# Moving and thinning the denominators' additions in the first attention of a fused attention and feed-forward kernel

## The chip, the core and the metric

The kernel runs on one core of a Trainium2 chip. A core has a matrix engine (TensorE, PE in the profile), a vector engine (VectorE, DVE), a scalar engine with table functions (ScalarE, ACT), a general engine (GpSimd, POOL) and SyncE (SP), which here only issues DMAs. Each engine takes its instructions in the order of its own list and meets the others through semaphores. The metric is device time in microseconds, the median of the runs. Lower is better.

## What is computed

There are 8 batches, 12 heads, 448 positions and a head dimension of 64. Queries and keys are normalised by their root mean square, and a softmax attention follows. Its output, 3584 tokens by 768, goes through a feed-forward layer of width 2048 with squared ReLU:

```
q_n, k_n = rmsnorm(q, g_q), rmsnorm(k, g_k)
attn = softmax(q_n @ k_n.T / sqrt(64)); x = attn @ v
h = x @ w_in; r = max(h, 0); out = (r * r) @ w_out
```

The two weight matrices come as 64-bit floats. The kernel turns them into 32-bit floats itself.

## The kernel before

**Stages.** The batches are taken two at a time, as a span. A span is one attention over 12 head pairs and then two products, each done as seven smaller block products in place of eight. The attention of a later span is woven into the second product of the span before it. Only the first attention (`attention_alone`) has no product to hide in: it stands alone at the start, and the first product of span 0 follows it.

**A head pair.** Each of the 12 pairs (`NAT`) goes through these steps. `load` brings q and k in from DRAM. `norm` squares them (ACT, L693), sums them (DVE, L694 and L695), takes the power -1/2 (POOL, L697) and multiplies q by it (POOL, L699). `transpose` turns k and then q on the PE (tile `pt`, L737), and ACT copies each result out (L739 for k, L741 for q). `scores` makes a chunk of 112 keys against all queries for both heads (PE, tile `sc`, L749), and ACT takes the exponential (L754). There are four chunks, 0 to 3. `values` multiplies the chunks by v (PE, tile `pav`, L805).

**The denominators.** The softmax needs the sum of the exponentials over the keys. `add_up` adds chunk 1 to chunk 0 and then chunk 2 to that (DVE, L764, 112 by 896 elements). `total_of` lets the PE multiply this sum, and each chunk that was not added, by a matrix of ones (tile `tot`, L815), which sums over the partitions. With three chunks added there are two operands, with two there are three. Each operand takes two matmul instructions, which the profile shows as four records. `finish` transposes the total, takes its reciprocal, transposes back and multiplies it into `pav` (DVE, L828, L829, L830, L835). `combine_x` makes the differences that the block products need (L845 to L850).

**The order.** It is written out by hand: each engine's list is the order in which the functions are called. In a pair the PE runs scores 0 and 1, the transpose of the next pair's k, the values of the pair before for chunks 2 and 3, the total of the pair before, the transpose of the next pair's q, scores 2 and 3, and the values for chunks 0 and 1.

**The weights' ticks.** At every `yield` of the attention the loop calls `weights`, which advances the conversion of the weights. One word of weights takes a tick of four quarters: a load (SP, L532), vector work (DVE, L588, L593, L598), scalar work (ACT, L575, L591), integer additions (POOL, L563) and block sums (POOL, L569). After every second word its seven blocks are written to a DRAM scratch of 1344 KB (`w1s`, SP, L583). `EARLY` says how many quarters are done by the end of the attention. The first product streams its stationary blocks `sw` back from that scratch (SP, L646); the first five of these loads are issued near the end of the attention, all on SP's one queue:

```
weights(min(EARLY, 4 + (EARLY - 4) * u // (4 * NAT - 7)))
if u == 4 * NAT - 9:
    load_blocks(5)
```

**Buffers.** `qk` holds two pairs of alternating parity, so `load(i + 3)` overwrites what `norm(i + 1)` has read. `tot` has one bank of PSUM, `pav` has two that alternate, and `pt` shares the bank of its predecessor: the transpose of q waits until ACT has copied the transpose of k.

Of the kernel before, what the change touches and what calls it, by code (L numbers as in the profile page):

```python
# [310 lines left out]
def load_q(nc, qk, q, i):  # L311

    _, H, S, D = q.shape
    b, h0 = divmod(2 * i, H)
    nc.sync.dma_start(places_of(qk, i, 0)[:S // 4, 0].rearrange("p (h e) -> p h e", h=2),
                      q[b, h0:h0 + 2].rearrange("h (p j) d -> p h (j d)", j=4))


def load_k(nc, qk, k, i):

    _, H, S, D = k.shape
    b, h0 = divmod(2 * i, H)
    dst = places_of(qk, i, 0)[:S // 4, 1].rearrange("p (j h d) -> p j h d", j=4, h=2)
    for h in range(2):
        nc.sync.dma_start(dst[:, :, h], k[b, h0 + h].rearrange("(p j) d -> p j d", j=4))
# [61 lines left out]
def attention_then_ffn_bounded(  # L387
# [41 lines left out]
    NJ = 4  # L429
    SP = S // NJ  # L430
    NPAIR = H // 2
    NFC = DFF // P
# [6 lines left out]
    NAT = 2 * NPAIR  # L439
# [16 lines left out]
    def bank(name, n=None):  # L456

        turn[0] += n is None
        return ps_m.tile([P, S], F32, tag="mn"[turn[0] % 2 if n is None else n], name=name)
# [22 lines left out]
    HW = HC * P  # L482
    WORDS, BLOCKS, EXPS = 7, 2, 4

    EARLY, ALL = 4 * 12, 4 * (2 * NFC + 3)
    assert DM == NW and BLOCKS * 8 * HW + EXPS * NW + 2 * NW <= 3 * HF * S and 2 * NW <= 4 * S and HF % 4 == 0


# [162 lines left out]
    vs, probs, pavs, tots, normed, rstds = {}, {}, {}, {}, {}, {0: rstd0}  # L651
# [3 lines left out]
    def load(i):  # L655
        if i < NAT:
            load_q(nc, qk, q, i)
            load_k(nc, qk, k, i)
            return

        b, h0 = i // NPAIR, 2 * (i % NPAIR)
        for s, src in enumerate((q, k)):
            dst = by_squares(i, 0)[:, s]
            for n in range(4):
                nc.sync.dma_start(dst[n * 32:(n + 1) * 32],
                                  src[b, h0 + n // 2, :, n % 2 * 32:n % 2 * 32 + 32]
                                  .rearrange("(g t) e -> t g e", t=32))

    def by_squares(i, work):
        n = i % 2 * 4 + 2 * work  # L670
        flat = qk[:, n:n + 2].rearrange("p n e -> p (n e)")[:, 0:2 * S]
        return flat.rearrange("p (s g e) -> p s g e", s=2, e=32)
# [11 lines left out]
    def norm(i):  # L684
        if i >= NAT:
            squares(i)
            return norm_by_squares(i)
        raw, sq = (places_of(qk, i, n)[:SP] for n in range(2))
        rstd = rstds[i] = small.tile([SP, 2, 2 * NJ], F32, tag="rstd", name="rstd", bufs=4)
        normed[i] = sq[:, 0], raw[:, 1]  # L690
        if i <= 2:
            return normalise_in_turn(nc, raw, sq, rstd, mhalf)
        nc.scalar.activation(sq, raw, AF.Square)  # L693
        nc.vector.tensor_reduce(rstd, sq.rearrange("p s (n d) -> p s n d", d=D), AX, ALU.add)  # L694
        nc.vector.tensor_scalar(rstd, rstd, 1.0 / D, 1e-6, ALU.mult, ALU.add)  # L695
        flat = rstd.rearrange("p s n -> p (s n)")
        nc.gpsimd.tensor_tensor(flat, flat, mhalf[:SP, 0:4 * NJ], ALU.pow)  # L697

        nc.gpsimd.tensor_tensor(sq[:, 0].rearrange("p (j h d) -> p h j d", j=NJ, h=2),  # L699
                                raw[:, 0].rearrange("p (h j d) -> p h j d", j=NJ, h=2),  # L700
                                rstd[:, 0].rearrange("p (h j) -> p h j ()", h=2).to_broadcast([SP, 2, NJ, D]),
                                ALU.mult)
# [30 lines left out]
    def transpose(i, s, n):  # L733

        pt = bank("pt", n)
        for j in range(NJ):
            nc.tensor.transpose(pt[:, j * SP:(j + 1) * SP], normed[i][s][:, j * P:(j + 1) * P], ident[:SP, :SP])  # L737
        if s:
            nc.scalar.copy(qkT[:, i % 2, s], pt)  # L739
        else:  # L740
            nc.scalar.activation(qkT[:, i % 2, s], pt, AF.Copy, scale=gains[:, 0:1])  # L741

    def scores(i, c):

        at = i % 2 if i < NAT else 0
        sc = ps_s.tile([SP, 2, 512], F32, tag="s", name="sc")
        for h in range(2):
            rows = slice(h * D, (h + 1) * D)
            nc.tensor.matmul(sc[:, h, 0:S], qkT[rows, at, 1, c * SP:(c + 1) * SP], qkT[rows, at, 0, :],  # L749
                             start=True, stop=True)  # L750
        pr = probs[i, c] = places[(NJ * i + c) % len(places)][:SP]
        if i < NAT:
            for h in range(2):
                nc.scalar.activation(pr[:, h], sc[:, h, 0:S], AF.Exp, scale=rstds[i][:, 1, 2 * c + h:2 * c + h + 1])  # L754
        else:
            nc.scalar.activation(pr, sc[:, :, 0:S], AF.Exp)  # L756

    def acc_of(i):
        return sums[i % 2] if i < NAT else sums["acc"]

    def add_up(i, c):

        acc = acc_of(i)[:SP]
        nc.vector.tensor_tensor(acc, probs[i, 0] if c == 1 else acc, probs[i, c], ALU.add)  # L764
# [35 lines left out]
    def values(i, chunks=range(NJ)):  # L800
        if 0 in chunks:
            pavs[i] = ps_o.tile([P, S], F32, tag="o", name="pav") if i >= NAT or i % 2 == 0 else bank("pav", 1)
        for c in chunks:
            for h in range(2):
                nc.tensor.matmul(pavs[i][h * D:(h + 1) * D, :], vs[i][:, h, c, :], probs[i, c][:, h, :],  # L805
                                 start=(c == 0), stop=(c == NJ - 1))

    def total_of(i):


        tots[i] = ps_o.tile([P, S], F32, tag="t", name="tot")
        parts = [acc_of(i)[:SP]] + [probs[i, c] for c in range(2 if i + 1 == NAT else 3, NJ)]
        for n, pr in enumerate(parts):
            for h in range(2):
                nc.tensor.matmul(tots[i][h * D:(h + 1) * D, :], sums["ones"], pr[:, h, :],  # L815
                                 start=(n == 0), stop=(n + 1 == len(parts)))

    def finish(i):

        b, hp = divmod(i, NPAIR)  # L820
        pav, factors = pavs.pop(i), xT[:, b % 2, hp]
        x = factors
        if i < NAT:


            turned, factors = sums["turned"], sums["factors"]
            few = small.tile([P, S // 32], F32, tag="few", name="few", bufs=1)
            nc.vector.transpose(turned, tots.pop(i))  # L828
            nc.vector.reciprocal(few, turned.rearrange("p (g r) -> p g r", r=32)[:, :, 0])  # L829
            nc.vector.transpose(factors.rearrange("p (g r) -> p g r", r=32),  # L830
                                few.rearrange("p g -> p g ()").to_broadcast([P, S // 32, 32]))

            x = x.rearrange("d (p j) -> d j p", j=NJ)
            pav, factors = (t.rearrange("d (j p) -> d j p", j=NJ) for t in (pav, factors))
        nc.vector.tensor_tensor(x, pav, factors, ALU.mult)  # L835
        del vs[i]
# [15 lines left out]
    def attention_alone():  # L852


        for i in range(NAT):
            more = i + 1 < NAT
            scores(i, 0)
            scores(i, 1)
            if i == 0:

                transpose(1, 1, 1)
                scores(0, 2)
                scores(0, 3)
                transpose(1, 0, 0)
                add_up(0, 1)
                add_up(0, 2)
                norm(2)
                load_v(1)
                values(0, (0, 1))
                load(3)  # L870
                yield
                continue
            if more:
                transpose(i + 1, 1, 0)
            if i + 3 < NAT:
                load(i + 3)
            values(i - 1, (2, 3))
            total_of(i - 1)
            add_up(i, 1)
            if i + 2 < NAT:  # L880
                norm(i + 2)
            elif not more:
                norm(NAT)
                load(NAT + 2)
            yield
            if more:
                transpose(i + 1, 0, 0)
            finish(i - 1)
            load_v(i + 1)
            yield  # L890
            scores(i, 2)
            scores(i, 3)
            values(i, (0, 1))
            yield
            if more:
                add_up(i, 2)
            combine_x(i - 1)
            if NAT <= i + 3 < NAT + 2:
                load(i + 3)
            yield  # L900
        values(i, (2, 3))
        total_of(i)
        finish(i)
        combine_x(i)
# [212 lines left out]
    for span in range(NSPAN):  # L1117
        more = span + 1 < NSPAN
# [108 lines left out]
```

## Time and profile before

| quantity | value |
|---|---|
| median of 3 runs | 1402.11 us (1399.25 to 1402.90) |
| the profiled execution | 1404.63 us |
| its span, first to last instruction | 1402.80 us |
| PE busy | 1378.1 us, 98% of the span |
| DVE, ACT, POOL busy | 814.3, 420.3, 590.7 us |
| first score matmul | 8.96 us |
| first matmul of the first product (tile `pa`) | 134.48 us |
| first score matmul of the second attention | 266.31 us |

Times inside the trace are counted from the span's start. In a row of the timeline the columns are start, duration, engine, line, operation, output and inputs, shape, count, and in brackets the engine's idle time before it with what ended it. Rows of equal instructions are merged with an x and a number. A share of busy time says little by itself; what counts is which wait ends last in each stage. From 266 us on the PE has no idle time, so the two stages before that are where the order of work can be seen in the time.

### The profile page before, as it was taken

The numbers are of one execution on the slowest core, as the hardware profiler recorded it, in microseconds if no ns is written. First come the engines' busy times: TensorE is split into PE (matmuls) and PEld (weight loads), VectorE is DVE, ScalarE is ACT, GpSimd is POOL, SyncE is SP. The second block draws the span as 40 slices with busy tenths as digits, with TensorE's granted clock in tenths as the row PEclk, the third lists the DMA queues.
The fourth block names the chain that finished last, engine by engine and source line by source line (L and its number), as shares of the span: only waits on it lengthen the run. The fifth ranks groups of instructions, "written<-read, shape, count | busy, mean of one in ns | idle before, by whom it ended". The sixth has DMA issues, their size and how long they took to land.

```text
span 1402.8 us, 14398 instructions
## 1 busy us (share of the span) xinstructions
PE 1378.1 (98%) x4426; PEld 635.5 (45%) x4426; DVE 814.3 (58%) x1404; ACT 420.3 (30%) x621; POOL 590.7 (42%) x400
## 2 busy tenths in 40 slices
PE   8989999999999999999999999999999999999997
PEld 3333444444444454544444455444444445554553
DVE  6989677589876234476767523457777633332111
ACT  7875555433322011233232011232323201110000
POOL 6998888544452022544353122445445302221000
PEclk9999999999999999999999999999999999999999
DMA  8676998645655333345565332344565343323443
GB/s 239 190 196 168 352 374 316 183 104 119 137 113 120 98 88 87 104 103 122 117 136 122 95 96 85 103 105 105 120 128 107 94 102 86 90 86 103 107 110 70
DMA packets 430914, 188.78 MB, mean 135 GB/s; under 512 B 277484, under 2 KB 428780, under 8 KB 430828
## 3 DMA queue, kind: packets, MB, share of 16 engines
q1 hardware_dynamic: 421228, 179.05, 49.3%
q10 hardware_dynamic: 9472, 8.72, 2.3%
q8 instruction: 37, 0.61, 0.2%
q14 instruction: 49, 0.40, 0.1%
q0 software_dynamic: 128, 0.00, 0.0%
HBM read 154.54 MB, written 33.16 MB: 134 GB/s over the span
## 4 chain that ended last, share of the span: by engine, by line
PE 89%; POOL 3%; DVE 3%; issue 1%; DMA 1%; ACT 1%; POOLq 0%; ACTq 0%
PE ps L1044 37%; PE pc L997 10%; PE pd L997 10%; PE pa L997 10%; PE sc L749 9%; PE pav L805 9%; PE pb L997 5%; DMA sw<-w1s 1%; DVE gT L764 1%; POOL rstd L697 1%; POOL gC L569 1%; POOL qk L699 1%; POOL gC L563 1%; DVE gC L598 0%; PE tot L815 0%
## 5 line engine op out<-in xcount | busy, mean ns | idle before, releaser
L1044 PE MATMUL ps<-gT,sw 128*128 128x448 f32 x768 | 299.2, 542 | 0.8 <-POOL gT L974 0.8
L719 POOL TENSOR_TENSOR half<-half,mhalf 128x28 f32<-128x28 f32 x36 | 173.6, 4824 | 262.3 <-DVE half L718 228.8
L1044 PE MATMUL ps<-gC,sw 128*128 128x448 f32 x576 | 225.2, 542 | 0.0
L974 POOL TENSOR_TENSOR gT<-gT 128x448 f32<-128x448 f32 x96 | 93.5, 976 | 311.9 <-ACT gT L970 311.9
L1044 PEld LDWEIGHTS ps<-gT,sw 128*128 128x128 f32 x768 | 143.9, 190 | 151.0 <-issue 146.5
L756 ACT ACTIVATE pr<-sc 112x896 f32<-112x896 f32 x120 | 104.8, 914 | 293.9 <-PE sc L749 201.7
L749 PE MATMUL sc<-qkT 64*112 64x448 f32 x768 | 171.5, 565 | 1.9 <-ACT gT L754 1.1
L1044 PEld LDWEIGHTS ps<-gC,sw 128*128 128x128 f32 x576 | 108.0, 190 | 112.3 <-issue 111.1
L997 PE MATMUL pa<-xT,sw 128*128 128x448 f32 x384 | 154.9, 539 | 0.5 <-DMA sw<-w1s 0.5
L970 ACT ACTIVATE gT<-gT 128x448 f32<-128x448 f32 x96 | 55.3, 576 | 312.6 <-DVE gT L1012 312.6
L749 PEld LDWEIGHTS sc<-qkT 64*112 64x112 f32 x768 | 61.2, 173 | 99.6 <-issue 81.5
L997 PEld LDWEIGHTS pa<-xT,sw 128*128 128x128 f32 x384 | 72.8, 190 | 72.5 <-issue 71.9
L805 PE MATMUL pav<-pr,vt 112*64 112x448 f32 x480 | 100.2, 547 | 0.0
L721 POOL TENSOR_TENSOR qk<-qk,half 128x448 f32<-128x448 f32 x72 | 84.3, 1191 | 2.8
L997 PE MATMUL pb<-xC,sw 128*128 128x448 f32 x192 | 77.6, 540 | 2.0 <-issue 1.5
L1012 DVE TENSOR_TENSOR gT<-z,pd 128x448 f32<-128x448 f32 x32 | 19.9, 621 | 102.2 <-PE pd L997 102.2
L764 DVE TENSOR_TENSOR acc<-acc,pr 112x896 f32<-112x896 f32 x60 | 68.3, 1138 | 18.4 <-ACT pr L756 15.9
L997 PE MATMUL pd<-xC,sw 128*128 128x448 f32 x192 | 77.5, 540 | 1.4 <-DMA sw<-w1s 1.3
L997 PE MATMUL pd<-xT,sw 128*128 128x448 f32 x192 | 78.0, 542 | 0.0
L997 PE MATMUL pc<-xC,sw 128*128 128x448 f32 x192 | 77.4, 539 | 0.0
L997 PE MATMUL pc<-xT,sw 128*128 128x448 f32 x192 | 77.4, 539 | 0.0
L569 POOL TENSOR_TENSOR gC<-gC 128x384 f32<-128x384 f32 x64 | 72.1, 1146 | 2.5
(120 smaller groups left out, 1565.7 us busy)
## 6 DMA issues: line engine op xcount, KB each, us to landing
sw<-w1s SPq DMA_DIRECT2D x224, 192.0 KB, 2.4
sw<-w2s SPq DMA_DIRECT2D x168, 256.0 KB, 3.3
w1s<-gC SPq DMA_DIRECT2D x8, 1344.0 KB, 7.5
w2s<-gC SPq DMA_DIRECT2D x8, 1344.0 KB, 5.7
out_dram<-osb SPq DMA_DIRECT2D x184, 56.0 KB, 1.9
qk<-in_q_dram SPq DMA_DIRECT2D x144, 56.0 KB, 3.0
qk<-in_k_dram SPq DMA_DIRECT2D x144, 56.0 KB, 2.9
vt<-in_v_dram SPq DMA_DIRECT2D x72, 112.0 KB, 2.9
```

What stands on the lines that cost most here:

```text
L569: nc.gpsimd.tensor_tensor(*[blocks_of(n)[:, i] for i in (dst, x, y)], op)
L719: nc.gpsimd.tensor_tensor(half, half, mhalf, ALU.pow)
L721: nc.gpsimd.tensor_tensor(qkn[:, s], raw[:, s], half[:, s * NG:(s + 1) * NG].rearrange("p g -> p g ()").to_broadcast([P, NG, 32]), ALU.mult)
L749: nc.tensor.matmul(sc[:, h, 0:S], qkT[rows, at, 1, c * SP:(c + 1) * SP], qkT[rows, at, 0, :], start=True, stop=True)
L756: nc.scalar.activation(pr, sc[:, :, 0:S], AF.Exp)
L764: nc.vector.tensor_tensor(acc, probs[i, 0] if c == 1 else acc, probs[i, c], ALU.add)
L805: nc.tensor.matmul(pavs[i][h * D:(h + 1) * D, :], vs[i][:, h, c, :], probs[i, c][:, h, :], start=(c == 0), stop=(c == NJ - 1))
L970: nc.scalar.activation(g, src, AF.Relu)
L974: nc.gpsimd.tensor_tensor(g, g, g, ALU.mult)
L997: nc.tensor.matmul(ps, stream[n + i][:, c], rhs[:, c], start=first and c == 0, stop=c == HC - 1, skip_group_check=not first)
L1012: add(g, x, ps, ALU.add)
L1044: nc.tensor.matmul(ps, stream[n][:, c % 4], rhs_of[i][:, c], start=c == 0, stop=c == HF - 1)
```

## The change

In the first attention, the DVE adds chunks 0 and 1 only for even pairs and for the last one, and chunks 0, 1 and 2 for the odd pairs; before, it added three chunks for all pairs but the last. The PE takes the third operand of `total_of` for those pairs. The total of a pair now comes after the next pair's scores 2 and 3, where it came before that pair's transpose of q, and `finish` follows after the values of chunks 0 and 1. The load of q and k three pairs ahead is called at the top of a pair. Thirteen ticks of the weights are done by the end of the attention instead of twelve.

```diff
-    EARLY, ALL = 4 * 12, 4 * (2 * NFC + 3)
+    EARLY, ALL = 4 * 13, 4 * (2 * NFC + 3)
...
+    def added(i):
+        return 3 if i % 2 and i + 1 < NAT else 2
+
     def total_of(i):
         tots[i] = ps_o.tile([P, S], F32, tag="t", name="tot")
-        parts = [acc_of(i)[:SP]] + [probs[i, c] for c in range(2 if i + 1 == NAT else 3, NJ)]
+        parts = [acc_of(i)[:SP]] + [probs[i, c] for c in range(added(i), NJ)]
...
             more = i + 1 < NAT
+            if 0 < i < NAT - 3:
+                load(i + 3)
             scores(i, 0)
             scores(i, 1)
...
                 add_up(0, 1)
-                add_up(0, 2)
                 norm(2)
...
                 transpose(i + 1, 1, 0)
-            if i + 3 < NAT:
-                load(i + 3)
             values(i - 1, (2, 3))
-            total_of(i - 1)
             add_up(i, 1)
...
                 transpose(i + 1, 0, 0)
-            finish(i - 1)
             load_v(i + 1)
             yield
             scores(i, 2)
             scores(i, 3)
+            total_of(i - 1)
             values(i, (0, 1))
+            finish(i - 1)
             yield
-            if more:
+            if added(i) == 3:
                 add_up(i, 2)
             combine_x(i - 1)
```

## The prediction

> **What bounds the kernel now.** I read the shares first, then the slices by stage, the waits of the first attention, the chain of waits, and the timelines of POOL and PE there. The page's shares and slices:
>
> ```profile
> PE 1378.1 (98%) x4426; PEld 635.5 (45%) x4426; DVE 814.3 (58%) x1404; ACT 420.3 (30%) x621; POOL 590.7 (42%) x400
> PE   8989999999999999999999999999999999999997
> ```
>
> PE is idle for only 24.7 us, nearly all in the first slices. The busy times by stretch (length, then each engine's time with its count, granted clock, DMA share, GB/s) say who competes with it there:
>
> ```profile
> 60.00:80.00 20.00, 19.50 (x104) 7.38 (x102) 19.73 (x25) 16.79 (x28) 19.69 (x13) 1.00 0.65 186
> 100.00:120.00 20.00, 16.48 (x82) 5.90 (x82) 19.13 (x27) 12.55 (x22) 19.68 (x12) 0.95 0.54 148
> 160.00:180.00 20.00, 19.52 (x52) 9.52 (x51) 15.18 (x20) 9.83 (x15) 17.18 (x18) 1.00 1.02 375
> 220.00:240.00 20.00, 20.00 (x55) 10.10 (x54) 14.03 (x18) 13.80 (x22) 16.84 (x18) 1.00 0.91 337
> ```
>
> In the attention PE, DVE and POOL are all full: a balance of three. In the first product the DMAs are full and PE waits little. The waits from 10 to 135 us (total, times, longest):
>
> ```profile
> PE tot L815 <- DVE gT L764: 4.4, 5, 1.5
> PE pt L737 <- POOL qk L699: 2.2, 2, 2.0
> PE sc L749 <- ACT gT L754: 1.1, 1, 1.1
> PE pav L805 <- DMA vt<-in_v_dram: 0.9, 1, 0.9
> ```
>
> The first row is what the change goes for. But the chain of waits, taken from 60 us on, is held by POOL from 67 to 116.5 us; its end is
>
> ```profile
> 110.71 3.06 POOL rstd L697
> 113.85 2.65 POOL qk L699
> 116.50 0.04 issue
> 116.55 0.60 PE pt L737 x4
> 117.15 2.26 PE sc L749 x8
> 119.41 2.73 PE pav L805 x8
> ```
>
> So the last multiplication of a norm (pair 11) releases the last transpose, and from there PE runs to the product at 134.48. POOL has three idle spells from 25.7 to 116.5 us: 0.54, 1.12 and crumbs. Its rows, and DVE's additions, show what fills it:
>
> ```profile
> 46.37 2.90 POOL L697 TENSOR_TENSOR rstd<-rstd,mhalf 112x16 f32<-112x16 f32 x1
> 49.36 1.04 POOL L699 TENSOR_TENSOR qk<-qk,rstd 112x512 f32<-112x512 f32 x1
> 69.88 1.86 POOL L699 TENSOR_TENSOR qk<-qk,rstd 112x512 f32<-112x512 f32 x1
> ```
>
> ```profile
> 70.74 1.95 DVE L764 TENSOR_TENSOR gT<-gT 112x896 f32<-112x896 f32 x1
> 78.22 1.07 DVE L764 TENSOR_TENSOR gT<-gT 112x896 f32<-112x896 f32 x1
> ```
>
> An addition takes 1.07 us alone and up to 1.98 beside POOL's elementwise work; POOL's multiplication takes 1.04 alone and up to 2.77. From 25 to 117 us POOL's four kinds of instruction take 28.4 + 16.0 + 24.0 + 20.8 = 89.2 us by the groups; at their shortest (9 x 2.9, 9 x 1.04, 16 x 1.01, 15 x 1.0) it would be 66.6. Collisions thus cost POOL some 22.5 us.
>
> **What the Trainium skill says.** "SBUF — State Buffer", section "SBUF: two separate sides": VectorE and GpSimd share a port pair under an exclusive lock, taken by a DVE instruction with two SBUF inputs or in a two-port mode, and the loser waits a whole instruction. The trace agrees (1.07 against 1.95 us above). "TensorE: Matmul & The Clock Gate", section "What's actually happening": the clock falls after an idle window. Here a 2.05 us wait is followed by 2.26 us of scores in place of 1.69, and 2.73 of values in place of 1.65: 1.65 us. "DMA: Bandwidth & Descriptors", section "Queues, rings and completion order": a DMA engine consumes a queue's descriptors in ring order. In the trace ScalarE waited until 84.29 us for a k load issued right behind the `w1s` write of 74.53: 9.76 us.
>
> **The change part by part.**
>
> *PE, more work.* Six pairs (0, 2, 4, 6, 8, 10) get a third operand: 24 records at 0.206 us (8 take 1.65) are +4.9 us. The totals' waits, 4.4 us, can go: a total now stands behind the next scores, so its sums have some 2.2 us more, and DVE has less to do. These two alone cancel.
>
> *PE, a lost cover.* The total used to stand between k's transpose and q's. The copy L739 (0.55) follows two exponentials (2.21) that begin 1.05 us after the scores; it ends at +3.7, and PE is back at +3.8 (1.69 + 0.53 + 1.65). Cover just suffices, except at the start: in pair 1 values end near 20.5, the copy at 22.5, a 2 us hole that the total filled. The norm too is needed 1.65 us earlier in the pair.
>
> *PE's floor.* From q's transpose at 22.58, pair 2 begins at 28.9; nine pairs take 9.4 or 10.2 in turn (5 x 9.4 + 4 x 10.2 = 87.8), so pair 11 begins at 116.7 and, with 13.2 to come, the product at 129.9: at best -4.6 us.
>
> *DVE.* Six additions go, 1.09 + 1.88 + 1.98 + 1.07 + 1.07 + 1.88 = 9.0 us; the tick adds 0.55 + 0.55 + 0.96 = 2.1. DVE then has slack. `finish` waits in DVE's list for a later total, with the ticks' vector work and the next additions behind it; those have a pair of slack, so I cost this at nothing. Were that cover gone, `finish` (2.5 us) would show once a pair.
>
> *POOL, the pacing engine.* Laid side by side, the instruction lists show four more POOL instructions ahead of pair 9's norm (two L563, two L569), never given back before pair 11's. At 1.01 us: +4.05. Idle that they fill (the 1.12): -1.1. Of the four additions removed by then (pairs 2, 4, 6, 8) three collided, 0.8 to 0.9 each: -2.6. The vector work of the extra quarters, 1.5 us, collides about half the time (22.5 us of loss against the stage's 42 us of DVE work in those forms: 18 additions, ten ticks' L588, L593 and L598, L845): +0.8. Sum +1.15: pair 11's multiplication ends at 117.65. Behind it PE now has 16.25 (before, at full clock) + 1.65 (the moved total of pair 9) + 0.8 = 18.7, against 17.93 measured with the slow clock: +0.77. Attention: +1.9. POOL's bounds: PE's floor (-4.6) below; above, four instructions at the stage's mean of 1.4 with no relief, +5.6 and so +6.4.
>
> *SP and DMA.* The top-of-pair load passes no other DMA; only ticks shift. The write of word 1 now stands ahead of load 7, that of word 5 no longer just ahead of load 11, whose late landing cost ScalarE 2.27 us at 104.06. I take these as even (each side up to 2). The write of word 9 (1344 KB) and one more word (768 KB) leave the product, and the first five `sw` loads now follow that write. It needs six POOL instructions after pair 11's multiplication, 6.1 to 8.1 us; with 9.8 us to land, `sw` is there 16 to 18 us after it, PE asks at 18.7. Covered by 1 to 3 us.
>
> *First product.* 56 blocks at 2.255 are 126.3 us of its 131.8. Waits at 149.0 (1.3, for `sw`), 163.4 (0.5, for `sw`) and 189.1 (0.6, DVE behind the weights' work) with their restarts cost 2.9; with one tick of 23 less I take two thirds: -1.9. The 1.46 at 138.5 is `finish` of pair 11 behind `combine_x`, and stays. Bounds: 0 and -3.
>
> Sum: +1.9 - 1.9 = 0 against the profiled 1404.63; the median lies 2.5 lower, 1402.1. I say 1402.0. Apart from this the PE is full after 266 us, and nothing there changes.
>
> **The rivals.**
> 1. *Gain.* Collisions fall further, since DVE is no longer full, and PE meets its floor: -4.6 - 2 = 1395.5. For it: the totals' waits are DVE's, and POOL's shortest times leave room. Against: POOL must end pair 11's norm at 111.2, 5.3 us sooner with four more instructions.
> 2. *POOL paces harder.* At pair 9's q transpose PE waits: seven L563/L569 (before: four) precede that power. With no relief +6.4, less 1.9 or a little less: 1407. It decides for slower (over 4.2 us) once pair 11's multiplication ends after 121.8 (116.5 + 4.2 + 1.9 - 0.8). For it: POOL hardly idles from 46 us. Against: three removed additions did collide.
> 3. *Given back at the product.* The attention ends 3 us sooner, but `sw`, behind word 9's write, is not there: PE waits, 1402 to 1403.
>
> **How the numbers follow.** Forecast 0.47 (own range 1398.5 to 1405), gain 0.22, POOL harder 0.20, given back 0.11. A measurement of this kernel can tell about 0.3%, 4.2 us. Faster 0.23: the gain and an edge of the forecast. Slower 0.20. Same 0.57: the rest. The 8-in-10 range runs from just above the gain's value to POOL's: 1396.5 to 1407.
>
> **What would show it.** Right: no wait of `tot` on L764; `pt` waiting for L699 around pairs 8 to 10; pair 11's L699 ending at 116 to 119; POOL without idle from 46 us; the product beginning within 3 us of 134.5, and lasting 129 to 131. Wrong: L699 waits gone and the product begun by 131 (gain); a wait of 3 us or more at pair 9 with a low clock after it (POOL); `pa` waiting for `sw` at the start (given back).

## The result, and the profile after

The changed kernel takes 1401.38 us (median of 4 runs, 1401.11 to 1404.00) beside 1401.44 us for the kernel before, a ratio of 1.0005 with a 95% interval of 0.9987 to 1.0023. Run again beside many more runs of the kernel before, it took 1404.14 against 1402.73 us, 1.0011 (1.0004 to 1.0019). That is the same within 0.3%; the interval says that the changed kernel is slower by 0.6 to 2.7 us. The forecast was 1402.0 us and no change.

Three parts of the change nevertheless move the time, in opposite directions, as the experiments show. First the views of the profile that answer to those of before.

The page's shares and PE's slices:

```profile
PE 1379.2 (99%) x4450; PEld 638.5 (46%) x4450; DVE 802.2 (57%) x1398; ACT 419.6 (30%) x621; POOL 581.7 (42%) x400
PE   8989999999999999999999999999999999999997
```

PE has the 24 records more that were counted, and DVE 6 instructions less. The busy times by stretch:

```profile
60.00:80.00 20.00, 19.50 (x102) 7.58 (x104) 17.16 (x23) 16.86 (x28) 19.76 (x13) 1.00 0.65 183
100.00:120.00 20.00, 19.67 (x106) 7.50 (x102) 17.66 (x22) 15.88 (x27) 19.76 (x12) 1.00 0.78 189
160.00:180.00 20.00, 20.00 (x55) 10.15 (x54) 13.62 (x19) 11.69 (x18) 16.83 (x17) 1.00 1.02 374
220.00:240.00 20.00, 20.00 (x55) 10.17 (x54) 13.80 (x18) 10.39 (x16) 15.80 (x16) 1.00 0.78 261
```

After the length come the busy times of PE, PEld, DVE, ACT and POOL. DVE fell from 19.7 to 17.2 us between 60 and 80 us, POOL stayed full, and PE is full in the product. Some rows of the waits from 10 to 135 us:

```profile
DVE gT L832 <- PE tot L819: 6.1, 6, 2.2
POOL rstd L697 <- PE sc L749: 4.6, 1, 4.6
PE pt L737 <- POOL qk L699: 4.4, 4, 2.3
PE pt L737 <- ACT qkT L739: 1.9, 1, 1.9
PE tot L819 <- DVE gT L832: 0.8, 1, 0.8
```

No total waits for an addition any more: 4.4 us gone. In their place stand 4.4 us of transposes waiting for the norm (2.2 before), the 1.9 us hole before pair 2's transpose of q, and 0.8 us of the last total waiting until DVE has read the one before it from the only bank. The first row is new too: `finish`, in DVE's list, now waits for the later total. The second row is POOL's power for pair 4, which starts late, at 35.37 us, behind such a wait of DVE. The chain of waits from pair 11's norm on:

```profile
110.57 2.87 POOL rstd L697
113.50 1.53 POOL qk L699
115.08 0.61 PE pt L737 x4
115.69 1.69 PE sc L749 x8
117.38 1.68 PE tot L819 x8
119.08 0.66 DVE gT L832
...
131.19 0.57 DVE gT L832
131.80 2.48 PE tot L819 x12
134.28 2.47 PE pa L1000 x6
```

POOL still releases the last transpose, at 115.0 us. From 119 us DVE holds the chain, up to the last total, though PE waited only 0.8 us for it. POOL's rows before pair 9's norm show the added instructions:

```profile
81.11 1.74 POOL L699 TENSOR_TENSOR qk<-qk,rstd 112x512 f32<-112x512 f32 x1
82.81 1.01 POOL L563 TENSOR_TENSOR gC<-words,gC 128x384 int32<-128x384 int32 x1
83.91 4.73 POOL L569 TENSOR_TENSOR gC<-gC 128x384 f32<-128x384 f32 x4
88.59 1.99 POOL L563 TENSOR_TENSOR gC<-words,gC 128x384 int32<-128x384 int32 x2
90.55 3.62 POOL L697 TENSOR_TENSOR rstd<-rstd,mhalf 112x16 f32<-112x16 f32 x1
94.25 1.04 POOL L699 TENSOR_TENSOR qk<-qk,rstd 112x512 f32<-112x512 f32 x1
```

Seven of them lie between two norms, and the transpose at 95.34 waited 2.25 us for the last row.

### The profile page after: what moved, and what is told of

Same layout as the page of the kernel before. It is cut to its first block, busy times and chain, and to the rows that moved or that the text cites. A ratio compares the mean times of both kernels' runs of the same rounds, so it can differ in the third digit from the quotient of the medians.

```text
span 1399.7 us, 14445 instructions
## 1 busy us (share of the span) xinstructions
PE 1379.2 (99%) x4450; PEld 638.5 (46%) x4450; DVE 802.2 (57%) x1398; ACT 419.6 (30%) x621; POOL 581.7 (42%) x400
## 4 chain that ended last, share of the span: by engine, by line
PE 93%; POOL 3%; DVE 1%; DMA 1%; ACT 1%; issue 1%; ACTq 0%; POOLq 0%
PE ps L1047 37%; PE sc L749 10%; PE pd L1000 10%; PE pa L1000 10%; PE pc L1000 10%; PE pav L805 9%; PE pb L1000 5%; PE tot L819 1%; POOL rstd L697 1%; POOL gC L563 1%; DMA sw<-w1s 1%; POOL gC L569 1%; PE pt L737 0%; ACT gT L754 0%; POOL qk L699 0%
## 5 line engine op out<-in xcount | busy, mean ns | idle before, releaser
L721 POOL TENSOR_TENSOR qk<-qk,half 128x448 f32<-128x448 f32 x72 | 81.3, 1150 | 2.8
```

The lines of the kernel that those rows point to most:

```text
L721: nc.gpsimd.tensor_tensor(qkn[:, s], raw[:, s], half[:, s * NG:(s + 1) * NG].rearrange("p g -> p g ()").to_broadcast([P, NG, 32]), ALU.mult)
```

## The experiments

Every kernel was compared with the kernel before on the same chip. The medians of before were 1402.73, 1402.74 and 1402.81 us in the three comparisons, each on another chip, so medians of different comparisons can be set side by side. By the intervals in the table, a median is known to about 1 us either way.

| kernel | additions | total and finish | ticks | median us | ratio to before (95%) | product begins at | product lasts |
|---|---|---|---|---|---|---|---|
| before, first trace | 3 chunks | old | 12 | | | 134.48 | 131.8 |
| before_again | 3 chunks | old | 12 | 1401.66 (one run) | | 132.39 | 131.2 |
| after, first trace | fewer | new | 13 | 1401.38 | 1.0005 (0.9987 to 1.0023) | 134.21 | 129.0 |
| again | fewer | new | 13 | 1404.14 | 1.0011 (1.0004 to 1.0019) | 134.53 | 129.8 |
| tick12 | fewer | new | 12 | 1403.84 | 1.0013 (1.0006 to 1.0019) | 133.92 | 130.8 |
| order_only | 3 chunks | new | 13 | 1408.96 | 1.0049 (1.0035 to 1.0062) | 142.15 | 129.1 |
| b_tick13 | 3 chunks | old | 13 | 1402.66 | 0.9999 (0.9991 to 1.0008) | 135.04 | 129.2 |
| thin_only | fewer | old | 12 | 1401.01 | 0.9990 (0.9984 to 0.9997) | 131.01 | 130.2 |
| thin13 | fewer | old | 13 | 1399.46 | 0.9976 (0.9969 to 0.9983) | 131.01 | 128.9 |
| thin14 | fewer | old | 14 | 1402.36 | 1.0000 (0.9992 to 1.0008) | 133.29 | 129.8 |
| total_back | fewer | total old, finish new | 13 | 1400.95 | 0.9985 (0.9978 to 0.9993) | 133.38 | 130.0 |
| fill | fewer | new, but pair 0's total old | 13 | 1402.31 | 0.9998 (0.9988 to 1.0007) | 135.36 | 129.0 |
| late | fewer | new, L699's work on DVE | 13 | 1405.77 | 1.0022 (1.0012 to 1.0032) | 139.04 | 128.2 |
| no_mult | fewer | new, L699 left out | 13 | 1400.52 | 0.9982 (0.9974 to 0.9989) | 134.46 | 129.2 |

The last two columns are of one profiled execution each, and the runs of one kernel differ by 2 us and more. For effects the medians decide; the traces say where time lies. Both traces of the changed kernel are faster than its median of 1404.14 us (1401.51 and 1402.65).

### The changed kernel again, and before again

Neither has an edit.

> The changed kernel once more, as the base for what is compared with it. If its 1401.4 us stand for themselves, the ratio to the kernel before lies within 0.998 to 1.002. In its trace the product should again begin near 134.2 us and last 129 us; if the 2.8 us by which the product was shorter came from run to run, its length should now be nearer to 131.

> The kernel before, for a second trace, since its first profiled execution lies 2 us above its median. If the 2.8 us by which the product is shorter after the change belong to the tick, the product lasts 131 to 132 us again; if they were chance, 129 to 130.5. The product should begin near 134.5 in either case, or 1 to 2 us sooner if the attention too was on the slow side.

The product lasted 131.8 and 131.2 us before, 129.0 and 129.8 after. In all traces of the table it lasts 130.2 to 131.8 us with twelve ticks and 128.2 to 130.0 with thirteen, so the shorter product is no chance. In the first trace of before the first eight score records took 3.33 us; in before_again, and in the first trace of the changed kernel, 1.76. PE's timeline, first of the first trace of before and then of before_again:

```profile
8.96 3.33 PE L749 MATMUL sc<-qkT 64*112 64x448 f32 x8 [0.77 <-ACT qkT L383]
```

```profile
9.02 1.76 PE L749 MATMUL sc<-qkT 64*112 64x448 f32 x8 [0.77 <-ACT qkT L383]
```

This row has 1.6 of the 2.1 us by which that attention was longer; the granted clock from 9 to 13 us was 0.58 there and 1.00 in before_again. Against the second trace, the changed kernel's attention is 1.8 to 2.1 us longer.

### One tick, in three settings

```diff
-    EARLY, ALL = 4 * 13, 4 * (2 * NFC + 3)
+    EARLY, ALL = 4 * 12, 4 * (2 * NFC + 3)
```

> The changed kernel with twelve ticks of the weights in the attention, as before the change. Theory (POOL paces the attention, the tick unloads the product): four POOL instructions less ahead of pair 9's norm, so the waits of the transposes for L699 (4.4 us in the changed kernel) fall to 1 us or less, the product begins 2 to 4 us earlier, near 131, and lasts 131 to 132 us again; in all within 2 us of the changed kernel. Rival (PE's own work paces the attention, the tick is free there): the product begins near 134 as now and lasts 131 to 132, so 2 to 3 us slower.

The time was as the theory had it (0.3 us from the changed kernel's), but not for its reason: the waits for L699 did not fall to 1 us. PE's timeline of tick12:

```profile
72.16 0.60 PE L737 MATMUL pt<-ident,qk 112*128 112x112 f32 x4 [2.21 <-POOL qk L699]
104.17 0.60 PE L737 MATMUL pt<-ident,qk 112*128 112x112 f32 x4 [3.01 <-POOL qk L699]
```

That is 5.2 us with four POOL instructions less. These waits stand at two L699 that collided, which is to say ran beside elementwise work of DVE and took longer (3.02 and 2.76 us for the two, 1.04 alone). So the number of POOL's instructions does not set the waits by itself.

In the kernel before, the tick was added alone:

```diff
-    EARLY, ALL = 4 * 12, 4 * (2 * NFC + 3)
+    EARLY, ALL = 4 * 13, 4 * (2 * NFC + 3)
```

> The kernel before with thirteen ticks, and nothing else of the change. Theory: with all additions on DVE, POOL's four more instructions make pair 9's to 11's transposes wait 3 to 6 us, the product begins at 137 to 140 and lasts 129 to 130: 1 to 3 us slower than before. Rival (the tick is free in the attention): the product begins near 134.5 and lasts 129: 2.5 to 3 us faster than before.

It made no difference (1402.66 us). In the trace the product begins at 135.04 us. The first scores took 3.33 us there, as in the first trace of before (134.48), so like with like the attention is 0.6 us longer. Its waits are other ones than expected; some rows from 10 to 145 us:

```profile
PE tot L815 <- DVE gT L764: 3.7, 4, 1.6
PE pav L805 <- DMA vt<-in_v_dram: 2.8, 1, 2.8
PE tot L815 <- DVE gT L828: 2.5, 1, 2.5
PE pt L737 <- POOL qk L699: 1.2, 2, 1.0
```

Only 1.2 us are POOL's; DVE has 6.2. One v load, issued at 80.76 us, landed 2.8 us after PE asked for it; on SP's queue it stands behind the write of word 3 (75.84) and a load of weights (79.53).

### Work taken from POOL

For `late` the multiplication of q moves from POOL to DVE, to the end of the pair:

```diff
-        nc.gpsimd.tensor_tensor(sq[:, 0].rearrange("p (j h d) -> p h j d", j=NJ, h=2),
+    def multiply(i):
...
+        nc.vector.tensor_tensor(sq[:, 0].rearrange("p (j h d) -> p h j d", j=NJ, h=2),
                                 raw[:, 0].rearrange("p (h j d) -> p h j d", j=NJ, h=2),
...
             combine_x(i - 1)
+            multiply(i + 2)
```

> The changed kernel with the multiplication of the norms 3 to 11 (L699, 1.04 to 1.75 us on POOL) on DVE, at the end of the pair, behind the combination. POOL has some 12 us less to do. Theory (POOL paces): no transpose waits for a norm any more, the attention comes down to PE's own work, the product begins at 130 to 131.5, in all 2.5 to 4 us faster than the changed kernel. Rival (PE paces): the product begins near 134 and nothing is gained; or DVE becomes the pace with 6 to 9 us more, and it is slower.

The theory fell here: 1.6 us slower than the changed kernel. PE's timeline of late:

```profile
98.23 0.98 PE L741 MATMUL pt<-ident,qk 112*128 112x112 f32 x4 [3.65 <-DVE qk L703]
120.99 0.57 PE L741 MATMUL pt<-ident,qk 112*128 112x112 f32 x4 [0.54 <-DVE qk L703]
```

The transposes wait for the same product on DVE, behind additions of 1.9 us, and it takes 1.3 to 1.5 us there. Only this one place in DVE's list was tried; another might cost less. For `no_mult` the multiplication is left out:

```diff
-        nc.gpsimd.tensor_tensor(sq[:, 0].rearrange("p (j h d) -> p h j d", j=NJ, h=2),
-                                raw[:, 0].rearrange("p (h j d) -> p h j d", j=NJ, h=2),
-                                rstd[:, 0].rearrange("p (h j) -> p h j ()", h=2).to_broadcast([SP, 2, NJ, D]),
-                                ALU.mult)
```

> The changed kernel with the multiplication of q by its norm (L699) left out for pairs 3 to 11, so that q goes unscaled (squared) into the scores: 10 to 13 us less for POOL, none more for DVE. Moving the same work to DVE had made the attention 4.5 us longer. Theory as mended (POOL and DVE together[...] are the pace): no transpose waits for a norm, the attention ends at PE's own work, the product begins at 130 to 131.5, 3 to 4 us faster than the changed kernel. Rival (ACT and PE are the pace, waits for L699 only take the place of others): the product begins at 133 or later and less than 1 us is gained.

The time fell by 3.6 us (1400.52 against 1404.14), as the mended theory had it. But in the trace the attention did not become shorter. Its waits from 10 to 145 us, PE's own:

```profile
PE tot L815 <- DVE gT L828: 2.2, 1, 2.2
PE pt L733 <- ACT qkT L735: 2.0, 1, 2.0
PE tot L815 <- DVE gT L760: 1.7, 1, 1.7
```

All of POOL's waits are gone, and DVE's took their place. That trace's run is 1.4 us above its median, so the two together suggest: removing 10 to 13 us of POOL's work gains 3 to 4 us, and DVE's lateness holds back the rest. The edit does two things, though: it takes work from POOL, and it lets q's transpose go without waiting for the norm. No run separates these. POOL then is one of two engines that set the pace, not the only one.

### The additions and the order, apart

The fewer additions alone, in the kernel before:

```diff
-        parts = [acc_of(i)[:SP]] + [probs[i, c] for c in range(2 if i + 1 == NAT else 3, NJ)]
+        parts = [acc_of(i)[:SP]] + [probs[i, c] for c in range(3 if i % 2 and i + 1 < NAT else 2, NJ)]
...
-                add_up(0, 2)
-            if more:
+            if more and i % 2:
                 add_up(i, 2)
```

> The kernel before with the fewer additions alone: old order, twelve ticks. Six additions go from DVE (9.0 us), 24 records come to PE (4.9 us). Theory: the totals' waits (4.4 us) mostly go and PE's work takes their place; POOL gains about 2.6 us of collisions; the product begins at 133 to 136, within 1.5 us of before. Rival (the extra matmuls are on the path with nothing in return): 4 to 5 us slower.

1.7 us faster than before: confirmed, a little beyond the 1.5 us stated. In the trace the totals' waits fell to 1.3 us, the transposes' to 1.2. From the first scores to the product PE is idle for 5.1 us (117.0 busy of 122.2), against 9.6 in before_again (113.8 of 123.4). The new order alone, with all additions (and thirteen ticks):

```diff
-        return 3 if i % 2 and i + 1 < NAT else 2
+        return 3 if i + 1 < NAT else 2
...
                 add_up(0, 1)
+                add_up(0, 2)
```

> The changed kernel with three chunks added for all pairs but the last, as before: new order and thirteen ticks, DVE with all its additions (9 us more than the changed kernel), PE without the 4.9 us. Theory: DVE and POOL are the pace, so with the additions back the transposes wait for L699 for 6 to 10 us where they wait 4.4 to 5 now, and PE's gain is used up: 0 to 3 us slower than the changed kernel. Rival (PE is the pace): 3 to 5 us faster than the changed kernel.

It is 4.8 us slower than the changed kernel, more than the 3 us that the theory allowed, and far from the rival. Some of its waits, from 10 to 145 us:

```profile
PE pt L737 <- POOL qk L699: 6.6, 4, 2.4
PE tot L819 <- DVE gT L832: 3.1, 1, 3.1
PE pt L737 <- ACT qkT L739: 2.0, 1, 2.0
```

Against b_tick13, which differs by the order alone, it is 6.3 us slower. With the fewer additions the same step costs 4.7 us at thirteen ticks (thin13, below, to the changed kernel) and 2.8 at twelve (thin_only to tick12). The order is the loss in all three. That it grows with the work on DVE and POOL fits these numbers, but their differences are hardly more than the medians can tell.

A large part of this loss isn't idle time. From the first scores to the product, first of b_tick13 and then of order_only:

```profile
8.95:135.04 126.09, 114.60 (x573) 42.34 (x573) 112.94 (x149) 96.40 (x159) 112.17 (x66) 0.99 0.83 225
8.90:142.15 133.25, 121.10 (x573) 45.70 (x573) 115.38 (x151) 97.08 (x159) 115.57 (x66) 0.92 0.79 214
```

The attention is 7.2 us longer with the same 573 records on PE, and 6.5 of these are longer busy time, at a granted clock of 0.92 in place of 0.99. PE is idle for only 0.7 us more. Waits that are followed by a slow clock thus cost more than their length.

### Which part of the order

Fewer additions and the tick, in the old order:

```diff
-    EARLY, ALL = 4 * 12, 4 * (2 * NFC + 3)
+    EARLY, ALL = 4 * 13, 4 * (2 * NFC + 3)
```

on top of thin_only.

> The kernel before with the fewer additions and thirteen ticks, in the old order: the changed kernel without its moved total, finish and load. Theory (the fewer additions gain 1.7 us, the tick gives 1.9 in the product and takes as much in the attention, the moved total costs 2.5 to 3 us): 1400.5 to 1402, 2 to 3.5 us faster than the changed kernel; the product begins near 132.5 and lasts 129. Rival (the additions' gain needs the new order once POOL has the tick's work too): near the changed kernel's 1404.

1399.46 us, faster than both kernels: 3.35 us below before, 0.9976 (0.9969 to 0.9983), and 4.7 us below the changed kernel. It beat the range expected by 1 us. Here the tick is worth 1.55 us (thin_only to thin13). Then the total alone goes back in the changed kernel:

```diff
             values(i - 1, (2, 3))
+            total_of(i - 1)
             add_up(i, 1)
...
             scores(i, 3)
-            total_of(i - 1)
             values(i, (0, 1))
```

> The changed kernel with its total back at the old place, ahead of the transpose of q; finish stays late and the load stays at the pair's top. Theory (the lost cover of the total ahead of the transpose is the cost): 1400.5 to 1402 as thin13, with no 1.9 us hole before pair 2's transpose and waits for L699 of 2 us or less in all. Rival (what costs is finish, late in DVE's list, with the additions and the norm's sums behind it): it stays within 1 us of the changed kernel, 1403.5 to 1404.5.

1400.95 us, 3.2 us better than the changed kernel: the total's place is the larger cost. Some waits of total_back, from 10 to 145 us:

```profile
POOL rstd L697 <- PE tot L819: 3.2, 2, 2.4
PE pav L805 <- DMA vt<-in_v_dram: 2.4, 1, 2.4
PE pt L737 <- POOL qk L699: 2.2, 2, 1.6
PE tot L819 <- DVE gT L764: 2.0, 1, 2.0
```

The 1.9 us hole is gone and L699 is waited for 2.2 us instead of 4.4. It stays 1.5 us above thin13, from which it differs by the later `finish` and the load's place. The load was not tried alone, and this trace doesn't show how the later `finish` costs its part. The first row is POOL's power waiting for a norm sum. The profile puts it down to PE's total, but DVE has no wait for a total there before 125 us; its own list is late, with the sum for pair 4 done at 34.60 us against 33.68 in thin13. In the first trace of the changed kernel, by contrast, `finish` did hold up what stands behind it, the additions and that sum, which ended at 35.29 (in its second trace the same wait is 0.60 us); DVE's row:

```profile
27.75 0.65 DVE L832 STREAM_TRANSPOSE gT<-tot 128x448 f32<-128x448 f32 x1 [2.24 <-PE tot L819]
```

The hole of pair 1 by itself:

```diff
             values(i - 1, (2, 3))
+            if i == 1:
+                total_of(0)
...
-            total_of(i - 1)
+            if i > 1:
+                total_of(i - 1)
```

> The changed kernel with the total of pair 0 alone back at its old place, in the 1.9 us hole of pair 1. If the path of the attention ran through that hole (PE's own work paces), 1.9 us and some 1.5 of slow clock go: 2 to 3.5 us faster than the changed kernel. If POOL and DVE pace the later pairs, the gain is given back at the transposes of pairs 7 to 11, whose waits for L699 grow from 4.4 us to 6 or more: within 1 us of the changed kernel.

1402.31 us, 1.8 us better than the changed kernel: nearer to the first case. The waits for L699 did grow, to 5.7 us in its trace, so part was given back; how much, one trace can't say. The gain itself stands in the medians alone: in the trace the product begins at 135.36 us, no sooner than in the changed kernel's two.

The tick's dose, in the old order with fewer additions:

```diff
-    EARLY, ALL = 4 * 13, 4 * (2 * NFC + 3)
+    EARLY, ALL = 4 * 14, 4 * (2 * NFC + 3)
```

> As thin13 with fourteen ticks. Theory: 1 to 2 us less in the product (it lasts 127.5 to 128.5, its waits being nearly gone), and 2 us or more in the attention, now that all ticks' POOL work stands ahead: within 1.5 us of thin13, rather slower. Rival (ticks are free in the attention when DVE has fewer additions): 1 to 2 us faster than thin13.

2.9 us slower than thin13. The attention ended 2.3 us later, as the theory had it, but the product was not shorter (129.8 us). In the trace the product of thin13 had little left to save; PE's waits of thin13 from 135 to 266 us (total, number, longest):

```profile
PE pb L996 <- issue: 1.5, 1, 1.5
PE pd L996 <- DMA sw<-w1s: 0.5, 1, 0.5
```

## Why the prediction was right, and where it was not

**The sum.** Forecast: attention +1.9, product -1.9, no change; the medians say +1.4 us. In the traces the product is 2.1 us shorter (129.0 and 129.8 against 131.8 and 131.2), and the attention 2 us longer than in the second trace of before; against the first it is equal, because that one had lost 1.6 us to a slow clock at its start. Pair 11's multiplication ended at 115.0 and 115.3 us, against 113.9 in before_again: +1.2 to +1.5, where the sum of POOL's terms had +1.15. The stated time 117.65, and the sign "116 to 119", were off because they were counted from the first trace.

That the sum came out is in part luck. Sorted by the parts of the change, its terms are -1.8 us for the fewer additions (-2.6 on POOL, +0.8 at the end), +1.85 for the tick (4.05 - 1.1 + 0.8 on POOL, -1.9 in the product), +1.65 for the order, and 1.65 of slow clock taken as gone. The medians give -1.7 for the additions, -1.55 for the tick and +4.7 for the order (thin_only, thin13, again). The additions were right; the tick was priced 3.4 us too high and the order 3.0 too low. With the steps in the other sequence, by way of tick12, the two misses are 1.6 and 1.2 us and again cancel. The slow clock was, moreover, probably subtracted twice: it belongs to the profiled execution, which was then lowered by 2.5 us to the median. In before_again the last transpose waits as long (2.06 us) and the scores after it take 1.69 us.

**PE's additional work and the totals' waits.** Right: 24 records more, no wait of a total for an addition. "These two alone cancel" leaves out POOL's relief, which has its own term: together the fewer additions gain 1.7 us (thin_only).

**"PE, a lost cover" failed.** It said that the cover just suffices except at the start, and the norm's earlier need was named without a price. The moved total costs 3.2 us (total_back against the changed kernel), where it had 1.65 at the end. 1.8 of them go with the hole of 1.9 us at the start (fill), which mattered. The other 1.4 (fill to total_back) go with transposes that wait longer for L699, whose lateness the total used to hide: 4.4, 4.9 and 5.7 us of waits in the traces with the total late, 2.2 in total_back.

**`finish` "at nothing" failed.** Each pair was said to have slack. The later `finish`, together with the load's place, costs 1.5 us (thin13 to total_back). In the changed kernel's trace DVE waits for totals 6 times, 6.1 us in all, and POOL's power for pair 4 is late behind one of these waits; in total_back no such wait is seen, so how the 1.5 us arise there stays open. The single bank of the total was not costed either: 0.8 us at the last total of the changed kernel, 3.1 in order_only.

**POOL as the pacing engine: half right.** It does release the last transposes, and to leave its multiplication out, and with it the transposes' wait for the norm, gains 3.6 us. But moving that work to DVE loses 1.6, and four POOL instructions less do not shorten the waits (tick12). What fits the runs best is that the pair of POOL and DVE is full, with their collisions; it is not shown apart from the rest. The Trainium skill ("SBUF — State Buffer", section "SBUF: two separate sides") has VectorE and GpSimd share a locked port pair; the durations seen agree (L699 took 1.04 us alone, and 3.02 from 69.08 us of tick12, where two additions of 1.13 us ran on DVE meanwhile), but no run here separates the port from the two engines' plain load.

**The tick.** Product -1.9: right in size. Its cost in the attention depends on the order: in all it is worth 1.55 us with the old order and fewer additions (thin13), nothing in the kernel before (b_tick13) and nothing in the changed kernel (tick12 is 0.3 us faster than it, less than the runs can tell).

**SP and DMA.** Right where it was priced: the first `sw` loads, behind word 9's write of 123.44, were there when PE asked at 134.2. The v loads behind the writes were not named: PE waited 2.2 to 2.8 us for one of them in b_tick13, thin_only, thin13 and total_back. It did so in before too (0.9 us, and 2.1 in before_again), and not in the changed kernel, so they are no part of its loss.

**The rivals.** Gain to 1395.5: no, PE's floor was not reached; even without L699 the attention stayed above it. POOL harder, 1407: not here; order_only, at 1408.96, comes near it, with waits for L699 (6.6 us) and for DVE (3.1) and a slow clock. Given back at the product by `sw`: no such wait.

## What to carry to other kernels

When several edits together change nothing, run them apart: here two of them gain 3.35 us and the third takes it back and more, and the version with the first two beats both kernels. Work of an engine that stands between two dependent steps is cover; before it is moved out of the way of one wait, ask which later arrival it hides, and who then stands in line behind the consumer that now waits longer. Where two engines are full together, moving work from one to the other can lengthen the stage (late); less work shortened it here (thin_only). A wait on PE can cost more than its length, so compare the busy time and the granted clock too, not the waits alone.

## What the runs showed of the hardware

A wait of some 2 us on PE is sometimes followed by a slower clock and sometimes not. In the changed kernel the 2.25 us wait at 95.34 us was followed by scores of 1.76 us, in its second trace the same wait (2.20 us at 93.93) by scores of 2.29 and a total of 2.84 in place of 1.72. The granted clock from 93 to 100 us was 1.00 in the one and 0.76 in the other; PE's rows, first of the one and then of the other trace:

```profile
95.87 1.76 PE L749 MATMUL sc<-qkT 64*112 64x448 f32 x8
```

```profile
94.46 2.29 PE L749 MATMUL sc<-qkT 64*112 64x448 f32 x8
96.68 2.84 PE L819 MATMUL tot<-gT,ones 112*64 112x448 f32 x8
```

The first scores of the program took 1.76 us in most traces and 3.2 to 3.3 in three (the first of before, b_tick13 and order_only). How often the slow clock comes depends on the kernel, too: over all runs the mean granted clock was 0.9983 in thin13, 0.9970 in the changed kernel (again), 0.9973 in b_tick13 and 0.9938 in order_only (0.9978 to 0.9983 in before, by chip). Times 1400 us, an estimate that holds only where PE sets the pace, that is 2.4, 4.2, 3.8 and 8.7 us lost: 1.8 of the 4.7 us by which thin13 beats the changed kernel, and nearly 5 of the 6.3 between b_tick13 and order_only.

A difference of 1.5 us between two traces of one kernel is as large as the effects sought here; a second trace of the kernel before was worth more than a closer reading of the first.
